# The written order of a feed-forward: GELUs and high halves behind the bank copies, another order of one pop, a second ring for one sum, low halves moved

## The chip, the core and the metric

The kernel runs on one core of a Trainium2 chip. A core has TensorE (PE; its weight loads are listed apart as PEld), VectorE (DVE), ScalarE (ACT), GpSimd (POOL) and SyncE (SP), each with its own in-order queue; they meet through semaphores. Matrix products go from on-chip memory (SBUF) into eight accumulation banks (PSUM) of 128 x 512 fp32 words. The metric is the device time of one execution in microseconds; lower is better.

## What is computed

One transformer block on 2048 rows of width 512, with a modulation vector that gives a shift, a scale and a gate for each of its two halves:

```python
x = A_x
sa, ca, ga, sb, cb, gb = silu(c) @ w_mod             # six vectors of 512
h = layernorm(x) * (1 + ca) + sa
x = x + ga * attention(h, k_cache, v_cache, wq, wo)  # 32 heads of 128, 512 keys
h = layernorm(x) * (1 + cb) + sb
x = x + gb * ((gelu(h @ w_gate) * (h @ w_up)) @ w_down)   # hidden width 1792
```

Inputs and outputs are fp32.

## The kernel before

**Precision.** TensorE works on fp16. Each fp32 operand is held as a *high half* (the value rounded to fp16) and a *low half* (the rest), and each product is three matmuls: low x high, high x high, high x low (`mm3`, L86, whose matmuls stand at L90). So every result that feeds another product costs ScalarE one copy to fp16 (the high half) and VectorE or GpSimd one subtraction (the low half).

**Stages.** Attention takes the first three quarters of the time. The feed-forward follows, in an order written out by hand: under `manual_schedule` each engine executes its instructions in the order in which the Python code emits them. The loop at the end of the kernel is that order (L1756 to L1777).

**The feed-forward's steps.** The hidden width is 14 tiles of 128 features, taken in pairs, and the rows are taken in two halves of 1024. That gives 14 values of n: 7 pairs for the first half of the rows (n = 0 to 6), then 7 for the second. Step q = 2n + m computes the gate projection (m = 0) or the up projection (m = 1) of pair n: two feature tiles by two blocks of 512 rows, four output tiles named "11", "12", "21", "22". It does so with seven block products instead of eight (a Strassen-like scheme), in the written order `ORDER` = 1, 2, 6, 7, 5, 4, 3. A *product* here is two groups of three matmuls into one bank. `CHAIN` (L865) tells the bank: products 1, 6, 7 and 4 pile up in bank a, 2 goes to bank b, 5 and 3 to bank c.

Since 1, 6, 7 and 4 add onto the same bank a, its state must be copied out between them: after 1 as "s1", after 6 as "u2", after 7 as "u3" (`keep`, a ScalarE copy at L885). The product that follows in bank a waits for that copy. Then VectorE adds: "11" = s1 + bank b, "22" = u3 + bank c after product 5, "12" = u2 + bank c after product 3 (L1270), and "21" is bank a itself after product 4.

**What becomes of the four tiles.** In a gate step (m = 0) each gets its GELU on ScalarE (`gelu`, L1276), straight after it is formed. In an up step (m = 1) VectorE multiplies gate by up (L1287). The result is the input of the down projection, in one of two forms:

- For n mod 7 in 5, 6 (`turned(n)` false) `parts` makes high and low halves of the four tiles (L1297, L1301) and the down projection is eight plain row blocks.
- For n mod 7 in 0 to 4 (`turned(n)` true) the down projection is again a seven-product scheme, and needs besides "11", "21", "22" four combinations: `sums_of` makes four subtractions on GpSimd (L1313), named t1, t3, t2, t4 in the order of the code, and then their high halves on ScalarE (L1297) and low halves on GpSimd (L1301).

**put_off and tick.** `put_off(n, fn)` lays a piece of work aside, and `tick()`, which runs once after each product, emits it at the n-th tick from then. Pieces due at the same tick come in the order in which they were laid aside. The counters given in `sums_of`, (high, low) = (2, 4), (3, 5), (3, 4), (4, 5), are such delays. Since `sums_of` is called in the last product of step 2n+1, a delay of 2 means behind the first product of step 2n+2, 3 behind its second, and so on.

**Pops.** The down projection's work is queued in `nexty`; `y_next()` takes a *pop* off it, six matmuls, at four places of a step: after the products 2, 6, 4 and 3 (k = 1, 2, 5, 6 in the loop). For a turned n, `yt_tasks` writes 14 groups of three matmuls, two times seven products in the order `YORDER`, and cuts them into seven pops. The pops of n begin in step 2n+2 after its third product: (1,2), (6,5), (7,3), (4,1'), (2',6'), (5',7'), (4',3'), a prime marking the second seven. They use banks ya, yb, yc by the same `CHAIN`, and behind every group VectorE adds the bank to an accumulator (`yt_add`, L1677, and L1680 where it is the first). A group that adds onto a bank waits for that read.

**Buffers.** `tmp` (L74) hands out tiles of a ring of six ("e"). In a gate step `place` gives such a tile to s1, u2 and u3, and the GELU of "21" takes one more; they are free again only when the low halves of t1 to t4, made in place of them, have been read, one gate step later. `place` has a test `k == 6`, but it is called with the names "s1", "u2", "u3".

**Others in the same queues.** During steps 2 to 6 the second half's layer norm runs beside the products (`ln_turned`): per 128 rows a normalization and a high half on ScalarE (L539, L543), a low half on GpSimd (L544), then a transposing DMA; `turned_out` writes its results with ScalarE and VectorE (L558, L559). During steps 8 to 13 `combos` makes the input combinations for the second half: high halves on ScalarE (L374), low halves and subtractions on GpSimd (L378, L574).

Of the kernel before, what the change touches and what calls it, by code (L numbers as in the profile page):

```python
# [10 lines left out]
F32 = mybir.dt.float32  # L11
# [4 lines left out]
ALU = mybir.AluOpType  # L16
AX = mybir.AxisListType

P = 128
# [6 lines left out]
QB = 512  # L26
# [38 lines left out]
def block_kernel(ctx: ExitStack, tc: tile.TileContext, x, kT, v, wq, wo, wg, wu, wd, cT, wc, wm, out):  # L65
    nc = tc.nc

    const = ctx.enter_context(tc.tile_pool(name="const", bufs=1))
    pool = ctx.enter_context(tc.tile_pool(name="pool", bufs=2))
# [4 lines left out]
    def tmp(name):  # L74
        return pool.tile([P, 512], F32, tag="e", name=name, bufs=NE)

    def raw(name):
        return pool.tile([P, 512], F32, tag="raw", name=name, bufs=NRAW)

    def pair(tag, name, bufs):  # L80
        return pool.tile([P, 2, 512], F16, tag=tag, name=name, bufs=bufs)
# [12 lines left out]
    def dma(out_, in_):  # L94
        moved[0] += 1
        nc.sync.dma_start(out_, in_)
# [81 lines left out]
    def col(name, i=0):  # L178
        return ST[name][:, i:i + 1]
# [113 lines left out]
    def turned(n):  # L293

        return n % NP < NP - NROW
# [159 lines left out]

    def put_off(n, fn):

        waits_.append([n, fn])

    def tick():  # L460
# [68 lines left out]
    def ln_turned(i):  # L529

        qb, i_ = divmod(i, QT)
        st = {}

        def load():
            st["x"] = raw("xs")
            dma(st["x"], y1[2 * QT + i])

        def norm():
            nc.scalar.activation(st["x"], st["x"], AF.Identity, bias=col("kinv", i), scale=col("kmax", i))  # L539

        def split():
            st["p"] = t = pool.tile([P, 2, W], F16, tag="p16", name="xh", bufs=NP16)
            nc.scalar.activation(t[:, 0, :], st["x"], AF.Copy)  # L543
            nc.gpsimd.tensor_tensor(t[:, 1, :], st["x"], t[:, 0, :], op=ALU.subtract)  # L544

        def turn():
            if i_ == 0:
                TURN[qb] = pool.tile([P, QT, 2 * KT, P], F16, tag="pt", name="xt", bufs=NPT)
            nc.sync.dma_start_transpose(TURN[qb][:, i_], st["p"].rearrange("p a b -> p (a b)"))

        return load, norm, split, turn
# [182 lines left out]
    def run(key):  # L734
        for fn in later.pop(key, []):
            fn()
# [130 lines left out]
    def with_posts(key, gen, bk, after):  # L867
        items = {}
        for k, (b, start) in CHAIN.items():
            g0, g1 = product(key, gen, k, bk(b), start, k in (2, 4, 3))  # L870
            items[k] = [g0, (g1[0], lambda k=k: after(k))]
        return items

    def banks(st, tags):
        def bk(k):
            def get():
                if k not in st:
                    st[k] = bank(*tags[k])
                return st[k]
            return get  # L880
        return bk

    def keep(st, k, t):
        st[k] = t
        nc.scalar.activation(t, st["a"], AF.Copy)  # L885

    def kept(k):
        return pool.tile([P, QB], F32, tag=k, name=k, bufs=1)
# [364 lines left out]
    NQ = 4 * NP  # L1253
# [7 lines left out]
    def f_scale(q):  # L1261
        return (q // 2) % NP * 2 + q % 2

    def f_items(q, hold=None):
        n, m = divmod(q, 2)
        st = {}
        done = set()

        def add(k, src):
            nc.vector.tensor_tensor(st[k], st[k], st[src], op=ALU.add)  # L1270

        def gelu(key, src):

            def apply():
                dst = tmp("fg") if key == "21" else src
                nc.scalar.activation(dst, src, AF.Gelu_apprx_tanh, scale=col("finv", f_scale(q)))  # L1276
                G[n, key] = dst

            return (apply,)

        def result(key, src):
            if m == 0:
                for step in gelu(key, src):
                    step()
            else:
                g = G[n, key]
                nc.vector.scalar_tensor_tensor(g, g, col("gsc", n % NP), src, op0=ALU.mult, op1=ALU.mult)  # L1287
                if not turned(n):
                    parts(key, G.pop((n, key)))
                elif key != "12":  # L1290
                    parts(key, g)
                else:
                    sums_of()

        def high_of(key, g):
            t = A[n, key] = pair("ot", "at", NOT)
            nc.scalar.activation(t[:, 0, :], g, AF.Copy)  # L1297

        def low_of(key, g, eng):
            t = A[n, key]  # L1300
            eng.tensor_tensor(t[:, 1, :], g, t[:, 0, :], op=ALU.subtract)  # L1301

        def parts(key, g):
            high_of(key, g)
            if key == "21":
                st["low"] = lambda: low_of(key, g, nc.vector)
            else:
                put_off(2, lambda: low_of(key, g, nc.vector))

        def sums_of():  # L1310
            g = {k: G.pop((n, k)) for k in ("11", "12", "21", "22")}
            for o, a, b in (("11", "12", "11"), ("12", "22", "12"), ("22", "22", "11"), ("21", "21", "22")):
                nc.gpsimd.tensor_tensor(g[o], g[a], g[b], op=ALU.subtract)  # L1313
            for key, o, high, low in (("t1", "11", 2, 4), ("t3", "12", 3, 5), ("t2", "22", 3, 4), ("t4", "21", 4, 5)):
                put_off(high, lambda key=key, o=o: high_of(key, g[o]))
                put_off(low, lambda key=key, o=o: low_of(key, g[o], nc.gpsimd))

        def out_(key, src):
            if not hold:
                result(key, src)  # L1320
            else:
                hold.append(gelu(key, src))

        def place(k):
            if m == 0:
                return pool.tile([P, QB], F32, tag="k", name="fg", bufs=2) if k == 6 else tmp("fg")
            return pool.tile([P, QB], F32, tag="p16", name="fu", bufs=NP16) if k == "s1" else kept(k)

        def after(k):
            done.add(k)  # L1330
            if k in (1, 6, 7):
                name = {1: "s1", 6: "u2", 7: "u3"}[k]
                keep(st, name, place(name))
            if k == 2:
                add("s1", "b")
                out_("11", st["s1"])
            elif k == 4:
                out_("21", st["a"])
            elif k == 3:
                if "low" in st:  # L1340
                    st["low"]()
                add("u2", "c")
                out_("12", st["u2"])
            if k in (5, 7) and {5, 7} <= done:
                add("u3", "c")
                out_("22", st["u3"])

        tags = {"a": ("s", "fa", 2) if q else ("qa", "fa", 1), "b": ("acc", "fb", NACC), "c": ("acc", "fc", NACC)}
        return with_posts(("f", q), 2 + q // (2 * NP), banks(st, tags), after)
# [168 lines left out]
    def items(g):  # L1518
        if g not in ITEMS:
            ITEMS[g] = q_items(g) if g < NG else f_items(g - NG, hold)  # L1520
        return ITEMS[g]
# [104 lines left out]
    def f_at(q, k, *fns):  # L1626
        at(("f", q, k), *fns)
# [8 lines left out]
    def step(q, fn):  # L1636
        f_at(q // 7, q % 7, fn)
# [9 lines left out]
    for p in range(2):  # L1647
        q = 61 + 14 * p
# [69 lines left out]
            del YR["t", qb]  # L1718

    ADDS = {1: ((0, 0),), 2: ((0, 0),), 6: ((0, 1),), 5: ((1, 1),), 7: ((1, 1),), 4: ((1, 0),), 3: ((0, 1),)}  # L1720
    YORDER = ((1, 2, 6, 5, 7, 3, 4), (1, 2, 6, 5, 7, 4, 3))
    LAST = {2: (0, 0), 7: (1, 1), 3: (0, 1), 4: (1, 0)}

    def yt_tasks(n):
        tasks = []
        for p in range(2):
# [21 lines left out]

            tasks += [(lambda k=k, f=group: f(k), lambda k=k, f=post: f(k)) for k in YORDER[p]]
        return [tasks[k:k + 2] for k in range(0, len(tasks), 2)]  # L1750
# [5 lines left out]
    for q in range(NQ):  # L1756
        n, m = divmod(q, 2)
        its = items(NG + q) if q < 2 else f_items(q)
        for k, pk in enumerate(ORDER):
            if (q, pk) not in f_done:  # L1760
                all_of(its[pk])
            run(("f", q, k))
            tick()
            if n and k == 2 and m == 0 and turned(n - 1):
                nexty += yt_tasks(n - 1)
            if k in ((1, 2, 5, 6) if q < NQ - 1 else (1, 5)):
                y_next()
        if m == 1 and not turned(n):
            for qi, (a, b) in enumerate((("11", "21"), ("12", "22"))):
                for i in range(QT):  # L1770
                    nexty.append(y_tasks((2 * (n // NP) + qi) * QT + i, [lambda n=n, a=a: A[n, a], lambda n=n, b=b: A[n, b]],
                                         [("f", n, 0), ("f", n, 1)], col("dysc", n % NP), f_final))
# [40 lines left out]
```

## Time and profile before

| | |
|---|---|
| time, median of 3 runs | 1762.55 us (1762.18 to 1762.99) |
| the profiled execution | 1762.83 us, its span 1761.0 us |
| granted TensorE clock, mean | 0.998 |
| feed-forward, step 2 to the last product | from 1359.5 us on |

How to read the lines that follow. A line of the timeline begins with its start in microseconds from the span's beginning and its length, then the engine, the source line, the operation, output<-input by the program's names, sizes, and how many instructions were merged; a bracket gives the idle time of that engine just before and what ended it. fa, fb, fc are the banks of a feed-forward product; ya, yb, yc those of a pop of a turned n, py those of a pop of rows; fg and u are the gate and up tiles, at the halves that feed the down projection, yt its accumulators, xs and xh the layer norm's tile and halves. A line of the waits names who waited for whom, the total in us, how often, and the longest. A line of a group has its count, busy time and mean in ns, and the idle time before its instructions with what ended it.

### The profile page before, as it was taken

The numbers are of one execution on the slowest core, as the hardware profiler recorded it, in microseconds if no ns is written. First come the engines' busy times: TensorE is split into PE (matmuls) and PEld (weight loads), VectorE is DVE, ScalarE is ACT, GpSimd is POOL, SyncE is SP. The second block draws the span as 40 slices with busy tenths as digits, with TensorE's granted clock in tenths as the row PEclk, the third lists the DMA queues.
The fourth block names the chain that finished last, engine by engine and source line by source line (L and its number), as shares of the span: only waits on it lengthen the run. The fifth ranks groups of instructions, "written<-read, shape, count | busy, mean of one in ns | idle before, by whom it ended". The sixth has DMA issues, their size and how long they took to land.

```text
span 1761.0 us, 26246 instructions
## 1 busy us (share of the span) xinstructions
PE 1718.3 (98%) x8020; PEld 788.1 (45%) x8022; DVE 1415.7 (80%) x2454; ACT 1242.6 (71%) x2797; POOL 1063.9 (60%) x1282
## 2 busy tenths in 40 slices
PE   7999999999999999999999999999999998999998
PEld 5444444444444444444444444444444343444443
DVE  7898898888888899888888888888876575656665
ACT  6988888888878777887778778787773544433342
POOL 4889777777788874745585584574512536642424
PEclk9999999999999999999999999999999999999999
DMA  7999999999999999999999999999985544743353
GB/s 238 216 203 212 212 217 204 224 215 215 218 213 228 205 208 185 206 212 234 209 202 240 219 198 229 208 216 206 212 152 159 137 144 151 181 142 98 96 154 97
DMA packets 690637, 339.83 MB, mean 193 GB/s; under 512 B 578880, under 2 KB 601408, under 8 KB 690496
## 3 DMA queue, kind: packets, MB, share of 16 engines
q1 hardware_dynamic: 690208, 337.63, 84.6%
q8 instruction: 63, 1.03, 0.2%
q14 instruction: 78, 0.64, 0.1%
q10 hardware_dynamic: 288, 0.52, 0.1%
HBM read 135.66 MB, written 61.87 MB: 112 GB/s over the span
## 4 chain that ended last, share of the span: by engine, by line
PE 83%; DVE 7%; ACT 5%; POOL 2%; issue 2%; DMA 1%; DVEq 0%; SPq 0%; POOLq 0%; ACTq 0%
PE py L90 19%; PE ps L90 17%; PE po L90 17%; PE qa L90 8%; PE fa L90 6%; PE qc L90 4%; PE fc L90 3%; PE ya L90 2%; PE qb L90 2%; PE fb L90 2%; ACT ee L991 1%; PE yc L90 1%; ACT p L1003 1%; PE pq L90 1%; DVE nm L982 1%
## 5 line engine op out<-in xcount | busy, mean ns | idle before, releaser
L991 ACT ACTIVATE ee<-ps,nm 128x512 f32<-128x512 f32 x512 | 349.8, 683 | 188.0 <-DVE nm L982 183.6
L1008 DVE SCALAR_TENSOR_TENSOR p<-ee,rr,p 128x512 f16<-128x512 f32 x512 | 459.0, 897 | 6.0 <-ACT p L1003 5.5
L982 DVE TENSOR_REDUCE nm<-ps 128x1 f32<-128x512 f32 x512 | 350.1, 684 | 105.0 <-PE ps L90 102.3
L90 PE MATMUL ps<-k,qt 128*128 128x512 f16 x1536 | 414.9, 379 | 5.6 <-ACT ee L991 4.5
L1003 ACT ACTIVATE p<-ee,rr 128x512 f16<-128x512 f32 x512 | 364.5, 712 | 23.4 <-DMA pt<-p 10.8
L90 PE MATMUL po<-pt,v 128*128 128x512 f16 x1536 | 372.9, 379 | 1.8 <-DMA pt<-p 1.8
L90 PE MATMUL py<-wo,ot 128*128 128x512 f16 x1536 | 371.5, 379 | 0.1
L90 PEld LDWEIGHTS <-w 128*128 128x128 f16 x2184 | 213.8, 98 | 272.6 <-issue 16.9
L90 PEld LDWEIGHTS <-v 128*128 128x128 f16 x1536 | 149.9, 98 | 184.1 <-DMA pt<-p 2.0
L90 PEld LDWEIGHTS <-ot 128*128 128x128 f16 x1536 | 150.2, 98 | 181.7 <-DVE ot L740 0.5
L90 PEld LDWEIGHTS <-qt 128*128 128x128 f16 x1536 | 145.9, 98 | 177.0 <-issue 4.5
L1313 POOL TENSOR_TENSOR fg<-fg 128x512 f32<-128x512 f32 x40 | 51.9, 1298 | 151.5 <-DVE fg L1287 149.1
L740 DVE SCALAR_TENSOR_TENSOR ot<-po,ot 128x512 f16<-128x512 f32 x128 | 87.7, 685 | 37.4 <-ACT ot L739 37.0
L1297 ACT ACTIVATE at<-fg 128x512 f16<-128x512 f32 x86 | 53.3, 626 | 79.2 <-DVE fg L1287 74.3
L991 ACT ACTIVATION_READ_ACCUMULATOR ee<-ps,nm 128x1 f32 x512 | 100.0, 195 | 0.0
L952 DVE SCALAR_TENSOR_TENSOR acc<-py,ysc,acc 128x512 f32<-128x512 f32 x128 | 94.7, 740 | 5.3 <-PE py L90 5.3
L90 PE MATMUL fa<-t,w 128*128 128x512 f16 x336 | 81.6, 379 | 11.2 <-ACT fg L885 10.2
L235 POOL TENSOR_TENSOR lw<-lw,half__86 128x1 f32<-128x1 f32 x37 | 22.9, 619 | 104.2 <-DVE lw L185 104.2
L90 PE MATMUL qa<-t,w 128*128 128x512 f16 x348 | 84.9, 379 | 0.0
L397 POOL TENSOR_TENSOR rs<-rs,nhalf 128x1 f32<-128x1 f32 x32 | 18.7, 584 | 101.9 <-DVE rs L391 99.0
L739 ACT ACTIVATE ot<-po 128x512 f16<-128x512 f32 x128 | 73.7, 576 | 5.0 <-PE po L90 5.0
L90 PE MATMUL ya<-at,wo 128*128 128x512 f16 x240 | 63.9, 382 | 6.5 <-DVE yt L1677 6.5
(241 smaller groups left out, 2765.2 us busy)
## 6 DMA issues: line engine op xcount, KB each, us to landing
w<-kept SPq DMA_DIRECT2D x123, 256.0 KB, 3.3
wo<-kept SPq DMA_DIRECT2D x70, 256.0 KB, 3.4
kept<-stage SPq DMA_DIRECT2D x61, 256.0 KB, 3.4
raw<-in_wo SPq DMA_DIRECT2D x56, 256.0 KB, 3.2
kept<-w SPq DMA_DIRECT2D x39, 256.0 KB, 3.4
rw<-in_wq SPq DMA_DIRECT2D x38, 256.0 KB, 3.1
hs<-hf SPq DMA_DIRECT2D x32, 256.0 KB, 2.8
pt<-p SPq DMA_TRANSPOSE x512, 3.5
```

What stands on the lines that cost most here:

```text
L90: nc.tensor.matmul(ps, a, b, start=first and n == 0, stop=last and n == 2, skip_group_check=chain)
L235: nc.gpsimd.tensor_tensor(out, out, half_, op=ALU.pow)
L397: nc.gpsimd.tensor_tensor(st["rs"], st["rs"], nhalf, op=ALU.pow)
L739: nc.scalar.activation(t[:, 0, :], src, AF.Copy, scale=scale)
L740: return lambda: nc.vector.scalar_tensor_tensor(t[:, 1, :], src, scale, t[:, 0, :], op0=ALU.mult, op1=ALU.subtract)
L952: nc.vector.scalar_tensor_tensor(acc[ti], st["p"], by, acc[ti], op0=ALU.mult, op1=ALU.add)
L982: nc.vector.tensor_reduce(nm, E[t]["ps"], axis=AX.X, op=ALU.max, negate=True)
L991: nc.scalar.activation(e, E[t]["ps"], AF.Exp, bias=E[t]["nm"], scale=1.0, accum_out=sm[:, t % 2:t % 2 + 1])
L1003: nc.scalar.activation(p16[:, 0, :], E[t]["e"], AF.Copy, scale=E[t]["r"])
L1008: nc.vector.scalar_tensor_tensor(p16[:, 1, :], E[t]["e"], E[t]["r"], p16[:, 0, :], op0=ALU.mult, op1=ALU.subtract)
L1297: nc.scalar.activation(t[:, 0, :], g, AF.Copy)
L1313: nc.gpsimd.tensor_tensor(g[o], g[a], g[b], op=ALU.subtract)
```

## The change

```diff
@@ put_off @@
+        if n == 0:
+            return fn()
         waits_.append([n, fn])
@@ ln_turned: split @@
             nc.scalar.activation(t[:, 0, :], st["x"], AF.Copy)
-            nc.gpsimd.tensor_tensor(t[:, 1, :], st["x"], t[:, 0, :], op=ALU.subtract)
+            put_off(2, lambda: nc.vector.tensor_tensor(t[:, 1, :], st["x"], t[:, 0, :], op=ALU.subtract))
@@ f_items: result @@
             if m == 0:
-                for step in gelu(key, src):
-                    step()
+                put_off(2 if key == "11" else 0, gelu(key, src)[0])
@@ f_items: parts @@
-                put_off(2, lambda: low_of(key, g, nc.vector))
+                put_off(3 if key == "11" else 2, lambda: low_of(key, g, nc.vector))
@@ f_items: sums_of @@
-            for key, o, high, low in (("t1", "11", 2, 4), ("t3", "12", 3, 5), ("t2", "22", 3, 4), ("t4", "21", 4, 5)):
-                put_off(high, lambda key=key, o=o: high_of(key, g[o]))
-                put_off(low, lambda key=key, o=o: low_of(key, g[o], nc.gpsimd))
+            late = 0 if n else 2
+            for key, o, high, low in (("t1", "11", 2, 5), ("t3", "12", 3, 6), ("t2", "22", 4, 5), ("t4", "21", 5, 6)):
+                put_off(high + (late if high < 5 else late // 2), lambda key=key, o=o: high_of(key, g[o]))
+                put_off(low + late // 2, lambda key=key, o=o: low_of(key, g[o], nc.gpsimd))
@@ f_items: place @@
-                return pool.tile([P, QB], F32, tag="k", name="fg", bufs=2) if k == 6 else tmp("fg")
+                return pool.tile([P, QB], F32, tag="k", name="fg", bufs=2) if k == "u2" and n else tmp("fg")
@@ the pops @@
-    YORDER = ((1, 2, 6, 5, 7, 3, 4), (1, 2, 6, 5, 7, 4, 3))
+    YORDER = ((1, 2, 6, 5, 7, 3, 4), (1, 2, 6, 7, 5, 4, 3))
@@ the loop of the feed-forward @@
-            if k in ((1, 2, 5, 6) if q < NQ - 1 else (1, 5)):
+            if k in ((1, 2, 5, 6) if q < NQ - 1 else (2, 5)):
                 y_next()
```

In words: the layer norm's low half moves from GpSimd to VectorE and two ticks back. In a gate step the GELU of "11" is emitted two ticks later, which is behind the copy u2. The high halves of t2 and t4 come one tick later, the low halves of all four too; for n = 0 the highs of t1, t3 and t2 come two ticks later still and the high of t4 and all lows one. The low half of "11" comes one tick later. u2 of a gate step gets a ring of its own, the two buffers "k" that held attention's keys (not for n = 0). In the second seven of a turned n the groups 5' and 7' change places. In the last step the first pop moves from behind product 2 to behind product 6.

## The prediction

> **What bounds the kernel now.** I read the page's busy shares first, then busy time by stretches, then the waits of the feed-forward, then its timeline.
>
> ```profile
> span 1761.0 us, 26246 instructions
> ...
> PE 1718.3 (98%) x8020; PEld 788.1 (45%) x8022; DVE 1415.7 (80%) x2454; ACT 1242.6 (71%) x2797; POOL 1063.9 (60%) x1282
> ```
>
> TensorE is the bound, so the change can only return time in which TensorE stands still or runs slowly. To find it I cut the feed-forward into periods: from product 1 of an even step q to product 1 of step q+2.
>
> ```profile
> 1359.48:1391.89 32.41, 29.20 (x127) 12.76 (x126) 19.07 (x29) 15.86 (x26) 13.00 (x11) 0.95 0.51 148
> 1391.89:1421.07 29.18, 27.67 (x127) 12.30 (x126) 19.46 (x29) 16.58 (x27) 14.13 (x12) 1.00 0.61 158
> 1421.07:1451.11 30.04, 27.68 (x128) 12.29 (x127) 22.23 (x33) 14.51 (x23) 11.51 (x9) 1.00 0.43 131
> 1451.11:1481.19 30.08, 27.52 (x128) 12.33 (x127) 20.73 (x30) 12.25 (x21) 15.51 (x12) 1.00 0.64 201
> 1481.19:1515.73 34.54, 29.42 (x127) 12.74 (x126) 18.64 (x28) 17.78 (x28) 25.78 (x21) 0.95 0.59 148
> 1515.73:1573.04 57.31, 57.14 (x266) 25.83 (x265) 33.98 (x46) 22.03 (x35) 28.12 (x21) 1.00 0.46 135
> 1573.04:1601.77 28.73, 27.51 (x127) 12.33 (x126) 17.78 (x27) 10.31 (x17) 9.54 (x8) 1.00 0.41 130
> 1601.77:1630.55 28.78, 27.52 (x128) 12.30 (x127) 18.49 (x28) 10.41 (x17) 9.54 (x8) 1.00 0.32 98
> ```
>
> The columns are the stretch and its length, then busy time (and count) of PE, PEld, DVE, ACT, POOL, then the granted clock. A product and a pop are six matmuls each, and six take 1.295 us (starts 1597.07 to 1598.37 and 1600.48 to 1601.77 in the rows below). A period with seven pops is 21 x 1.295 = 27.2 us; the stretch from 1515.73 holds two with eight pops each, 57.0. So the periods lose 5.2 (q=2), 2.0 (q=4), 2.85 (q=6), 2.9 (q=8), 7.35 (q=10), 0.3 (q=12 to 15), 1.55 (q=16) and 1.6 us (q=18; I take q=20, 22, 24 to be alike). With the last step's 1.1 that is about 29.6 us: all there is to win.
>
> ```profile
> PE fa L90 <- ACT fg L885: 14.7, 14, 3.4
> ...
> ACT fg L885 <- POOL at L1301: 8.0, 3, 5.0
> ...
> PE ya L90 <- DVE yt L1677: 6.5, 10, 0.7
> ...
> PE fa L90 <- ACT u L885: 1.0, 1, 1.0
> ```
>
> Two waits fill it: products wait for ScalarE's copy of bank a (L885), and pops wait for a VectorE add (L1677). Printed idle is some 0.16 us below the lost time, since a matmul's modelled end overlaps the next start; I count from start to start.
>
> **The pop order** (YORDER). Around a pop of step 17:
>
> ```profile
> 1597.07 0.81 PE L90 MATMUL yc<-at,wo 128*128 128x512 f16 x3
> ...
> 1597.72 0.81 PE L90 MATMUL ya<-at,wo 128*128 128x512 f16 x3
> ...
> 1598.37 1.46 PE L90 MATMUL fc<-b,w 128*128 128x512 f16 x6
> 1598.83 0.74 DVE L1680 TENSOR_SCALAR yt<-yc,dyc 128x512 f32<-128x512 f32 x1
> 1599.67 0.75 DVE L1677 SCALAR_TENSOR_TENSOR yt<-ya,dyc,yt 128x512 f32<-128x512 f32 x1
> ...
> 1600.48 0.81 PE L90 MATMUL ya<-at,wo 128*128 128x512 f16 x3 [0.65 <-DVE yt L1677]
> ```
>
> Group 5 (yc) and group 7 (ya) are followed by group 4, which adds onto bank a and so waits until VectorE has read 7. TensorE was ready at 1598.37+1.295 = 1599.66 and lost 0.81. Swapped, 7's add takes the place at 1598.83 and lets group 4 go at 1598.83+0.81 = 1599.64: no wait. Group 3 is late next: it adds onto bank c, whose read now runs 1599.67 to 1600.42, so it starts at 1600.48 instead of 1600.31. The loss goes from 0.81 to 0.17, ten times: 6.4 us (between 0, if the adds fall further behind, and 8.1).
>
> **GELU and high halves behind the copies.** Step 18:
>
> ```profile
> 1601.77 1.46 PE L90 MATMUL fa<-b,w 128*128 128x512 f16 x6
> 1602.55 5.31 POOL L1313 TENSOR_TENSOR fg<-fg 128x512 f32<-128x512 f32 x4 [19.00 <-DVE fg L1287]
> ...
> 1605.35 0.72 ACT L1276 ACTIVATE fg<-fg,finv 128x512 f32<-128x512 f32 x1 [0.86 <-DVE fg L1270]
> ...
> 1605.98 1.20 ACT L1297 ACTIVATE at<-fg 128x512 f16<-128x512 f32 x2
> ...
> 1607.09 0.58 ACT L885 ACTIVATE fg<-fa 128x512 f32<-128x512 f32 x1
> ...
> 1607.72 1.46 PE L90 MATMUL fa<-t,w 128*128 128x512 f16 x6 [0.61 <-ACT fg L885]
> 1607.82 4.50 POOL L1301 TENSOR_TENSOR at<-fg,at 128x512 f16<-128x512 f32 x4
> ```
>
> POOL's subtractions start at P = 1602.55, 1.33 apart. ScalarE's queue is GELU, high of t3, high of t2, copy u2; t2's high waits for the third subtraction (P+3.99 = 1606.54), the copy follows at 1607.09 and product 7 at P+5.17. TensorE could have gone at 1601.77+4x1.295 = 1606.95. Afterwards only t3's high stands ahead of the copy, and waits for the second subtraction: P+2.66 = 1605.21, copy 0.55 later, product 7 another 0.63 later, P+3.84 = 1606.39. P hangs on VectorE's queue, in which the pop swap exchanges two adds of one length, so P stays while TensorE comes 0.64 earlier: 0.08 is left. This period goes from 1.6 to 0.08+0.17 = 0.25, and so four times: 5.4 us. In q=16 no such pop stands before it, and only the 0.17 stays: 1.4.
>
> The GELU then runs where ScalarE waits for TensorE, and its result is used a step later. The low halves stay covered: POOL ends four subtractions at P+5.3 and two lows at P+7.6, while the pop with groups 6 and 5 needs t2's low in its third matmul, P+3.84+3x1.295+0.43 = P+8.15. That is a slack of 0.55 us; uncovered, each microsecond of lag costs one per period.
>
> **The second ring.** Of the three waits of the copy u3 for POOL's lows (8.0 us), 5.0 lie in q=10 and the others in q=4 and 6. The tmp ring has six buffers and held four tiles of each n; with u2 elsewhere it holds three, so u3 no longer meets a tile whose low half is pending. What is left in q=4, 6 and 8 is the bound by P.
>
> ```profile
> 1421.79 5.72 POOL L1313 TENSOR_TENSOR fg<-fg 128x512 f32<-128x512 f32 x4 [7.80 <-DVE fg L1287]
> ...
> 1451.89 6.02 POOL L1313 TENSOR_TENSOR fg<-fg 128x512 f32<-128x512 f32 x4 [18.36 <-DVE fg L1287]
> ```
>
> I leave 0.25 in q=4, 0.5 in q=6 and 0.8 in q=8, because the four subtractions last 0.4 (q=6) and 0.7 us (q=8) longer than 5.31, and half of that lies ahead of t3's high. Gains: 1.75, 2.35, 2.1.
>
> **The layer norm's low half goes to VectorE.**
>
> ```profile
> L544 POOL TENSOR_TENSOR xh<-xs,xh 128x512 f16<-128x512 f32 x8 | 9.2, 1155 | 16.3 <-ACT xh L543 11.5 <-issue 4.7
> ...
> L1301 DVE TENSOR_TENSOR at<-fg,at 128x512 f16<-128x512 f32 x43 | 30.7, 714 | 0.7
> ...
> L1270 DVE TENSOR_TENSOR fg<-fg,fc 128x512 f32<-128x512 f32 x26 | 17.9, 687 | 45.5 <-PE fc L90 35.0 <-ACT fg L885 10.5
> ```
>
> Eight times 1.16 us leave POOL and eight times 0.71 enter VectorE, 5.7 us, beside 45.5 us in which it idles ahead of one add alone. Bounds 0 and 5.7; I take 0.5, for step 5, where this half, the moved low of "11" and a layer-norm output all come ahead of the add of u3. The low of "11" elsewhere only shifts within that idle time.
>
> By the Trainium skill (GPSIMD Engine Reference, section 8, Key points) GpSimd shares its SBUF interfaces with VectorE and contends with VectorE instructions that have two SBUF inputs, which the moved half is: it would stretch the subtractions of q=4 and q=6, some 0.3 us each by my estimate, and the sum would be 0.6 worse. The trace bears it out only as far as the subtractions' lengths differ (5.31 in q=18).
>
> **The first pop of sums** (n=0, q=2):
>
> ```profile
> 1362.21 5.31 POOL L1313 TENSOR_TENSOR fg<-fg 128x512 f32<-128x512 f32 x4 [4.61 <-DVE fg L1287]
> ...
> 1366.75 0.58 ACT L885 ACTIVATE fg<-fa 128x512 f32<-128x512 f32 x1
> ...
> 1367.38 1.48 PE L90 MATMUL fa<-t,w 128*128 128x512 f16 x6 [2.56 <-ACT fg L885]
> ...
> 1368.67 2.74 PE L90 MATMUL fc<-t,w 128*128 128x512 f16 x6
> ```
>
> The copy again trails t2's high, and behind the stall six matmuls take 2.54 us (1368.67 to 1371.21), half speed: 2.7 of the 5.2 us are the wait, the rest the clock and one pop wait. With the highs two pops later, products 7, 5 and 4 run unhindered from 1359.48+4x1.295 = 1364.66, and the pop with groups 6 and 5 is due at 1368.55. Now t2's high is late: it stands behind the GELU of "22", which needs product 5 (ends near 1367.4), an add and itself 0.7 each: high 1368.9 to 1369.5, low on POOL until 1370.7, third matmul due at 1368.98. It loses 1.75, with the swap's 0.17 1.9 in all: 3.3 us gained.
>
> **Step 10**, where POOL also makes the next block's combinations:
>
> ```profile
> 1491.91 2.27 POOL L1301 TENSOR_TENSOR at<-fg,at 128x512 f16<-128x512 f32 x2
> ...
> 1493.10 0.60 ACT L885 ACTIVATE fg<-fa 128x512 f32<-128x512 f32 x1 [5.02 <-POOL at L1301]
> ...
> 1494.14 1.16 POOL L378 TENSOR_TENSOR t<-cb,t 128x512 f16<-128x512 f32 x1
> ...
> 1495.09 1.49 PE L90 MATMUL ya<-at,wo 128*128 128x512 f16 x3
> ```
>
> The ring's 5.0 us go, but the same lows are what the pop at 1495.09 reads. They move one tick back, behind the L378 of 1494.14 (1.1 us): t2's low ends at 1491.91+1.1+2.3 = 1495.3. TensorE, unhindered, is there at 1481.19-0.64+7x1.295+0.08 = 1489.7, its third matmul at 1490.1: a stall of 5.2 us, and half speed behind it (three matmuls in 1.49 against 0.81 now; 3.4 us at half speed are 1.7). Loss 7.2 after 7.35: next to nothing gained.
>
> By the Trainium skill (TensorE: Matmul & The Clock Gate, Part 1) the clock halves after one idle window of about 3.4 us on a free-running grid. The trace shows half speed after a wait of 2.56 already, so I charge it; by the rule a stall of 5.2 covers a whole window only about half the time, an estimate, and the sum would be 0.9 better.
>
> **The rest.** Steps 12 to 15: 0.3, as the copy no longer follows the GELU. Last step: its second pop moves between products 6 and 7 and covers the copy (1.0 printed): 1.1.
>
> **Sum**: 5.4 + 1.4 + (1.75 - 0.5) + 2.35 + 2.1 + 3.3 + 0.15 + 0.3 + 1.1 = 17.3 us, so a span of 1743.7. The profiled execution took 1762.83, 1.8 over its span and 0.3 over the median of the runs: 1745.
>
> **Rivals.**
> (a) Step 10's stall does not come, because POOL passes its combinations faster when the layer norm is off it: 6.9 more, 1738. For it: 5 us of ring wait vanish. Against it: POOL is busy 25.78 of 34.54 us there, and the layer norm's halves are mostly gone by then.
> (b) The copies stay tied to P+5.2, because VectorE brings the second subtraction or the GELU's input later; then the pop swap is swallowed too, and only n=0, the ring, steps 12 to 15 and the last step pay: some 6 us, 1756. Against it: the GELU is no longer ahead of the copy.
> (c) Slower: t2's low, moved back a tick, comes late at the pop with groups 6 and 5 in all eight ordinary periods. The slack is 0.55; with a lag of 3.5 us beyond it and half speed behind each stall (1.7), 8 x 5.2 - 17 = 24 us lost, 1787; it decides from a lag of about 2.7 (2.1 us a period, before the clock). For it: step 10 shows POOL's queue doing this once. Against: the other periods have POOL busy 9.5 to 15.5 us of 30.
> (d) No effect that can be told: the second ring could be a dead test, as the old one is (place gets "u2", never 6), but the new one compares names, and the swaps are plain.
>
> **Chances**: forecast 0.70, (a) 0.12, (b) 0.11, (c) 0.05, (d) 0.02. The forecast's own spread, from 0 to 8.1 for the swap, 0 to 5.7 for the halves and 0 to 1.7 for a clock drop in q=2, is about 1740 to 1750; (a) takes the range down to 1738, part of (b) up to 1753. A measurement here tells 0.2%, 3.5 us, from no change: faster 0.93, same 0.02, slower 0.05.
>
> **What would show it.** Right: the ten waits of ya on L1677 gone or replaced by about 0.0 to 0.2 ahead of yc; product 7 at P+3.8 in steps 18 to 24, the wait for L885 down from 14.7 to 2 or less; no L885 waiting on L1301; one wait of ya near step 10 on POOL's L1301 of about 5 us, with the clock at half behind it; in step 2 one of 1 to 2 us in the pop. Wrong: product 7 still at P+5, a new wait of pops on L1301 in ordinary periods, or VectorE late at the add of u3.

## The result and the profile after

The changed kernel takes 1748.13 us (median of 4 runs, 1746.52 to 1749.16), the kernel before 1762.77 us (4 runs, 1762.18 to 1763.44): 14.6 us less. The ratio is 0.9916 with a 95% interval of 0.9899 to 0.9933. The prediction was 1745, with a range of 1738 to 1753. The profiled execution took 1748.16 us, its span 1745.9 us, so 15.1 us of span went.

The waits of TensorE in the feed-forward of the changed kernel, all that the view lists (who waited for whom, us in total, times, longest). Lines of the source have moved by up to two: L887 is the copy of bank a, L1302 the low halves, L1298 the high halves.

```profile
PE ya L90 <- POOL at L1302: 5.7, 2, 5.1
PE ya L90 <- ACT at L1298: 0.8, 1, 0.8
PE fa L90 <- ACT fg L887: 0.8, 3, 0.3
PE fa L90 <- ACT u L887: 0.4, 1, 0.4
```

The 14.7 us of waiting for the copy are 0.8, the ten waits for VectorE's add are gone from the list, and one wait of 5.1 us for a low half on GpSimd is new. Busy time by the same stretches as before (product 1 of an even step to product 1 two steps on):

```profile
1360.43:1389.58 29.15, 27.67 (x127) 12.33 (x126) 20.80 (x31) 15.54 (x26) 9.59 (x8) 1.00 0.57 162
1389.58:1417.34 27.76, 27.51 (x127) 12.33 (x126) 21.74 (x33) 16.47 (x27) 10.34 (x8) 1.00 0.64 166
1417.34:1445.36 28.02, 27.68 (x128) 12.32 (x127) 23.59 (x34) 14.29 (x23) 10.66 (x8) 1.00 0.50 141
1445.36:1473.16 27.80, 27.51 (x127) 12.33 (x126) 20.77 (x30) 12.37 (x21) 15.52 (x12) 1.00 0.67 210
1473.16:1507.84 34.68, 29.58 (x127) 12.77 (x126) 18.68 (x28) 18.13 (x28) 25.20 (x21) 0.90 0.59 144
1507.84:1565.19 57.35, 57.21 (x266) 25.82 (x264) 34.34 (x47) 21.92 (x35) 28.30 (x21) 1.00 0.48 140
1565.19:1592.55 27.36, 27.35 (x127) 12.34 (x126) 17.26 (x26) 10.40 (x17) 9.55 (x8) 1.00 0.41 130
1592.55:1619.99 27.44, 27.43 (x128) 12.31 (x126) 18.54 (x28) 10.40 (x17) 9.56 (x8) 1.00 0.34 101
```

The first number after the stretch is its length. Every period but that of step 10 and the long one has moved closer to the 27.2 us that its 21 groups of six matmuls need. The gains, before minus after: 3.3 (step 2), 1.4, 2.0, 2.3, -0.1 (step 10), 0.0 (steps 12 to 15), 1.4 (step 16), 1.3 in each of the four periods from step 18 to step 25. From step 26 to the end it is 0.5. That is 16.0 us; 0.95 are lost before step 2 (it begins at 1360.43 instead of 1359.48), where the change moves no more than one low half. In the kernels run below that start lies between 1359.5 and 1361.7; the kernel with the pop order alone, which changes nothing ahead of step 2, begins it at 1360.73.

The timeline of the changed kernel around a pop and the step behind it:

```profile
1589.79 1.46 PE L90 MATMUL fc<-b,w 128*128 128x512 f16 x6
1590.25 0.75 DVE L1682 TENSOR_SCALAR yt<-ya,dyc 128x512 f32<-128x512 f32 x1
1591.09 0.81 PE L90 MATMUL ya<-at,wo 128*128 128x512 f16 x3
1591.10 0.75 DVE L1679 SCALAR_TENSOR_TENSOR yt<-yc,dyc,yt 128x512 f32<-128x512 f32 x1
...
1591.90 0.81 PE L90 MATMUL yc<-at,wo 128*128 128x512 f16 x3
...
1592.55 1.46 PE L90 MATMUL fa<-b,w 128*128 128x512 f16 x6
...
1593.98 5.33 POOL L1314 TENSOR_TENSOR fg<-fg 128x512 f32<-128x512 f32 x4 [18.27 <-DVE fg L1288]
...
1596.64 0.63 ACT L1298 ACTIVATE at<-fg 128x512 f16<-128x512 f32 x1 [0.72 <-POOL fg L1314]
...
1597.17 0.58 ACT L887 ACTIVATE fg<-fa 128x512 f32<-128x512 f32 x1
...
1597.81 1.46 PE L90 MATMUL fa<-t,w 128*128 128x512 f16 x6
1597.99 0.63 ACT L1298 ACTIVATE at<-fg 128x512 f16<-128x512 f32 x1 [0.24 <-POOL fg L1314]
1598.53 0.70 ACT L1278 ACTIVATE fg<-fg,finv 128x512 f32<-128x512 f32 x1
```

Group 4 (ya, 1591.09) starts 1.30 behind product 3, so without a wait. Group 3 (yc, 1591.90) starts 0.81 behind it instead of 0.65: the read of bank c by the add at 1591.10 costs it 0.16. On ScalarE the copy (1597.17) stands right behind the high half of t3, and the high half of t2 and the GELU follow it. Product 7 comes at 1597.81, which is P+3.83 with P = 1593.98.

In step 12 a copy that prepares an accumulator's transpose (L1698) stands ahead of the copy of bank a, and product 7 starts 1.60 behind the pop's 1513.09 instead of 1.295:

```profile
1513.09 1.46 PE L90 MATMUL py<-wo,at 128*128 128x512 f16 x6
1513.11 1.05 ACT L1698 ACTIVATE yu<-yt 128x1024 uint16<-128x1024 uint16 x1
...
1514.06 0.58 ACT L887 ACTIVATE fg<-fa 128x512 f32<-128x512 f32 x1
...
1514.69 1.46 PE L90 MATMUL fa<-t,w 128*128 128x512 f16 x6
```

### The profile page after: what moved, and what is told of

It is laid out like the page before. It is cut to its first block, busy times and chain, and to the rows that moved or that the text cites. A ratio compares the mean times of both kernels' runs of the same rounds, so it can differ in the third digit from the quotient of the medians.

```text
span 1745.9 us, 26253 instructions
## 1 busy us (share of the span) xinstructions
PE 1716.3 (98%) x8022; PEld 787.6 (45%) x8022; DVE 1423.4 (82%) x2462; ACT 1243.0 (71%) x2797; POOL 1056.9 (61%) x1274
## 4 chain that ended last, share of the span: by engine, by line
PE 85%; DVE 5%; ACT 4%; POOL 2%; DMA 2%; issue 1%; SPq 0%; POOLq 0%; DVEq 0%; ACTq 0%
PE py L90 19%; PE po L90 17%; PE ps L90 17%; PE qa L90 8%; PE fa L90 7%; PE qc L90 4%; PE fc L90 4%; PE ya L90 2%; PE qb L90 2%; PE fb L90 2%; DMA pt<-p 1%; PE yc L90 1%; ACT ee L993 1%; ACT p L1005 1%; PE pq L90 1%
## 5 line engine op out<-in xcount | busy, mean ns | idle before, releaser
L742 DVE SCALAR_TENSOR_TENSOR ot<-po,ot 128x512 f16<-128x512 f32 x128 | 87.8, 686 | 36.7 <-ACT ot L741 36.3
L1298 ACT ACTIVATE at<-fg 128x512 f16<-128x512 f32 x86 | 53.9, 627 | 88.8 <-DVE fg L1288 75.0
```

The source lines that it names most:

```text
L742: return lambda: nc.vector.scalar_tensor_tensor(t[:, 1, :], src, scale, t[:, 0, :], op0=ALU.mult, op1=ALU.subtract)
```

## The experiments

Two theories were to be told apart. By the *chain*, product 7 is tied to P, the start of the subtractions, and P to VectorE; the parts of the change then only work together. By the rival, each part removes its own wait and the gains add up. Lengths of the periods in us (start of product 1 to start of product 1; 27.2 is the least, 57.0 for the long one), from the profiles:

| period from step | 2 | 4 | 6 | 8 | 10 | 12 to 15 | 16 | 18 |
|---|---|---|---|---|---|---|---|---|
| before | 32.4 | 29.2 | 30.0 | 30.1 | 34.5 | 57.3 | 28.7 | 28.8 |
| after | 29.15 | 27.8 | 28.0 | 27.8 | 34.7 | 57.35 | 27.4 | 27.4 |
| pop order alone | 30.1 | 29.2 | 30.0 | 30.1 | 34.5 | 57.95 | 28.1 | 28.8 |
| after, old pop order | 29.8 | 28.0 | 28.0 | 28.0 | 34.85 | 57.0 | 28.0 | 28.0 |
| after, without second ring | 31.1 | 28.5 | 29.2 | 28.8 | 36.3 | 57.3 | 27.4 | 28.15 |
| after, old GELU and halves | 30.1 | 29.1 | 31.7 | 31.8 | 33.45 | 58.0 | 28.1 | 28.8 |
| after, layer norm's halves back | 29.3 | 29.35 | 28.8 | 27.8 | 35.4 | 57.3 | 27.4 | 27.4 |
| after, late = 0 | 28.7 | 27.75 | 28.0 | 27.8 | 34.1 | 57.35 | 27.4 | 27.4 |
| after, lows of n=4 on VectorE | 29.15 | 27.75 | 28.0 | 27.8 | 28.9 | 57.3 | 27.4 | 27.4 |
| the same, t2's high earlier | 28.7 | 27.75 | 28.0 | 27.8 | 29.1 | 57.35 | 27.4 | 27.4 |

### The pop order alone

```diff
 # the kernel before
-    YORDER = ((1, 2, 6, 5, 7, 3, 4), (1, 2, 6, 5, 7, 4, 3))
+    YORDER = ((1, 2, 6, 5, 7, 3, 4), (1, 2, 6, 7, 5, 4, 3))
```

> The kernel before with the new pop order alone (5' and 7' exchanged), nothing else of the change. Theory of the chain: product 7 of a gate step is bound by P, the start of GpSimd's subtractions, and P hangs on VectorE, which the swap does not shorten. So TensorE gains 0.64 us at each of ten pops and gives it back at product 7 in all periods whose sums follow; only the pops of n=4 and n=11 keep it: 1.3 us, about 1761.4. The wait of ya for L1677 goes, the wait of fa for L885 grows from 14.7 to about 20 us, product 7 stays at P+5.2 in steps 18 to 24. Rival, the parts add up: ten times 0.64 to 0.81, 6.4 to 8.1 us, 1755 to 1756, with the wait for L885 unchanged.

Measured: 1762.00 us against 1762.84 for the kernel before; ratio 0.9998, interval 0.9989 to 1.0007. The waits of TensorE and step 18 of this kernel:

```profile
PE fa L90 <- ACT fg L885: 20.4, 14, 3.9
...
1602.13 5.31 POOL L1313 TENSOR_TENSOR fg<-fg 128x512 f32<-128x512 f32 x4 [19.00 <-DVE fg L1287]
...
1607.31 1.46 PE L90 MATMUL fa<-t,w 128*128 128x512 f16 x6 [1.26 <-ACT fg L885]
```

No wait for an add is left, the wait for the copy has grown from 14.7 to 20.4 us, and product 7 stands at P+5.18. The wait before it is 1.26 where it was 0.61. P has not moved with TensorE: it lies 1.43 us behind product 1 (1600.70), where it lay 0.78 behind it. The periods of steps 4, 6, 8, 10 and 18 are what they were to a tenth; that of step 16, with no new pop ahead of it, keeps 0.64, and the long period ahead of step 16 is 0.64 longer. The 2.3 us of step 2 are for the most part half speed that the profile of before has and this one has not (shown in the last section). The sum theory falls.

### The changed kernel with the old pop order

```diff
 # the changed kernel
-    YORDER = ((1, 2, 6, 5, 7, 3, 4), (1, 2, 6, 7, 5, 4, 3))
+    YORDER = ((1, 2, 6, 5, 7, 3, 4), (1, 2, 6, 5, 7, 4, 3))
```

> The changed kernel with the old pop order. Theory of the chain: with the copies no longer behind the GELU the swap is worth 0.56 us in each ordinary period (0.81 lost against 0.08 plus 0.17), 0.64 for n=4 and n=11, nothing where step 10 follows: about 5.2 us, 1753.3. Product 7 in steps 18 to 24 comes without a wait. Rival, the parts add up: the same 6.4 to 8.1 as alone, 1754.5 to 1756. The two theories part by the difference to the swap alone: 1.3 against 5.2 for the chain, equal for the rival.

Measured: 1751.46 us, ratio to the kernel before 0.9938 (0.9925 to 0.9950), 3.3 us slower than the changed kernel. The intervals of the two ratios overlap; the lowest of the runs here, 1750.78, lies above the highest of the changed kernel, 1749.16. Step 18:

```profile
1596.19 5.33 POOL L1314 TENSOR_TENSOR fg<-fg 128x512 f32<-128x512 f32 x4 [18.27 <-DVE fg L1288]
...
1600.59 1.46 PE L90 MATMUL fa<-t,w 128*128 128x512 f16 x6
```

Product 7 has no wait at all here, and steps 18 to 24 take 28.0 instead of 27.4 us: 0.57 each, against 0.56 expected. Steps 2 and 16 lose 0.65 each, but steps 4, 6 and 8 only 0.25, 0.0 and 0.2, where the slower subtractions leave the rest of the gain to P, and the long period is even 0.4 shorter: behind n=4 the swap is not kept. That is why the sum stays below 5.2. So one and the same edit is worth nothing that can be told alone (0.8 us between the medians) and 3.3 us with the rest.

### The changed kernel without the second ring

```diff
 # the changed kernel, place(), m == 0
-                return pool.tile([P, QB], F32, tag="k", name="fg", bufs=2) if k == "u2" and n else tmp("fg")
+                return tmp("fg")
```

> The changed kernel with u2 of the gate steps in the common ring of six again. Theory of the chain: copy u3 then waits in every period for the low half of t1 on GpSimd, which now ends near P+6.5 while the copy would be due at P+5.4; product 4 comes at P+7.1 instead of P+6.4. Seven periods with 0.7 us, 4.9 us, about 1753; the wait of fa for L885 near 5 to 6 us, L885 waiting for L1301's low on GpSimd in each gate step. Rival: the ring only mattered where the kernel before showed the wait, in steps 4 and 6: 1.4 us, 1749.5.

Measured: 1757.53 us, ratio to before 0.9968 (0.9955 to 0.9980), 9.4 us slower than the changed kernel. Step 18:

```profile
1599.64 5.33 POOL L1314 TENSOR_TENSOR fg<-fg 128x512 f32<-128x512 f32 x4 [18.36 <-DVE fg L1288]
...
1606.12 0.60 ACT L887 ACTIVATE fg<-fa 128x512 f32<-128x512 f32 x1 [1.22 <-POOL at L1302]
...
1606.77 1.46 PE L90 MATMUL fa<-t,x 128*128 128x512 f16 x6 [0.55 <-ACT fg L887]
```

The copy u3 waits for a low half on GpSimd, and product 4 comes at P+7.13 (P+7.1 expected): 0.7 us in steps 4 and 18 to 24, 1.2 and 1.0 in steps 6 and 8. The ring is thus more than a remedy for the three waits that the profile of before showed: it is what lets the later low halves be late. The expectation was still too small: it left out step 2 (31.1 against 29.15), where u3 of n=1 needs the tile of n=0 whose low comes late on purpose, and step 10 (36.3 against 34.7), where product 4 waits 6.3 us for the copy. Steps 6 and 8 are dearer than the 0.7 reckoned, too.

### The changed kernel with the old places of GELU and halves

```diff
 # the changed kernel
-                put_off(2 if key == "11" else 0, gelu(key, src)[0])
+                put_off(0, gelu(key, src)[0])
...
-            late = 0 if n else 2
-            for key, o, high, low in (("t1", "11", 2, 5), ("t3", "12", 3, 6), ("t2", "22", 4, 5), ("t4", "21", 5, 6)):
+            late = 0
+            for key, o, high, low in (("t1", "11", 2, 4), ("t3", "12", 3, 5), ("t2", "22", 3, 4), ("t4", "21", 4, 5)):
```

> The changed kernel with the GELU of 11 and the halves of t1 to t4 emitted where they were before (also for n=0); pop order, second ring, layer norm's low half and low half of 11 as changed. Theory of the chain: product 7 is back at P+5.2 (1.33 us in seven periods, 0.8 in step 16) and step 2 loses 3.3: 13.4 us, about 1761.5, so that nearly the whole gain goes although three of the parts stay. Rival, the parts add up: only the waits for L885 of before come back, some 9 to 11 us, 1757 to 1759, and the pop order's 6.4 us stay.

Measured: 1763.58 us, ratio to before 1.0000 (0.9991 to 1.0009). Step 18, and product 7 of step 8:

```profile
1603.97 5.32 POOL L1314 TENSOR_TENSOR fg<-fg 128x512 f32<-128x512 f32 x4 [19.00 <-DVE fg L1288]
...
1606.12 0.72 ACT L1278 ACTIVATE fg<-fg,finv 128x512 f32<-128x512 f32 x1 [0.22 <-DVE fg L1272]
...
1607.97 0.63 ACT L1298 ACTIVATE at<-fg 128x512 f16<-128x512 f32 x1 [0.61 <-POOL fg L1314]
...
1609.14 1.46 PE L90 MATMUL fa<-t,w 128*128 128x512 f16 x6 [1.26 <-ACT fg L887]
```

```profile
1459.18 2.63 PE L90 MATMUL fa<-t,w 128*128 128x512 f16 x6 [2.55 <-ACT fg L887]
```

Pop order, second ring and layer norm's halves are as changed, and nothing of the gain is left: product 7 is again at P+5.2 (1.26 us of wait in step 18) and the periods of steps 16 and 18 are those of the pop order alone. Steps 6 and 8 are even 1.7 us longer than before; their waits reached 2.5 us and matmuls at half speed followed. Without these 3.4 us this kernel would lie some 2.6 us below the kernel before, whose own profile has 1.7 us of the kind in step 2. The lines also tell which of the moved pieces holds up the copy: the high half of t2 waits for the third subtraction until 1607.97, when the GELU has been over for more than a microsecond. GELU and high halves were not run apart.

### The layer norm's low halves back on GpSimd

```diff
 # the changed kernel, split()
-            put_off(2, lambda: nc.vector.tensor_tensor(t[:, 1, :], st["x"], t[:, 0, :], op=ALU.subtract))
+            nc.gpsimd.tensor_tensor(t[:, 1, :], st["x"], t[:, 0, :], op=ALU.subtract)
```

> The changed kernel with the layer norm's low halves on GpSimd again, at their old place. Theory: GpSimd then has one such half of 1.16 us ahead of the lows of t1 and t2 in steps 2 and 6 and two in step 4, with a slack of 0.55 us: the pop with groups 6 and 5 waits 1.75 us in step 4, 0.6 in step 6, 0.3 more in step 2, in all 2.6 us slower than the changed kernel, about 1750.8. Rival, as the record has it: the move only costs VectorE time (0.5 us in step 5) and saves nothing, so that undoing it gives 1747.6.

Measured: 1750.23 us, ratio to before 0.9926 (0.9914 to 0.9939), 2.1 us slower than the changed kernel. Step 4:

```profile
1397.87 1.16 POOL L546 TENSOR_TENSOR xh<-xs,xh 128x512 f16<-128x512 f32 x1 [0.24 <-ACT xh L545]
...
1398.98 4.50 POOL L1302 TENSOR_TENSOR at<-fg,at 128x512 f16<-128x512 f32 x4
1401.31 0.38 PE L90 MATMUL ya<-at,wo 128*128 128x512 f16 x1 [1.82 <-POOL at L1302]
```

The third matmul of the pop waits 1.8 us for t2's low; the periods of steps 4 and 6 are 1.6 and 0.8 us longer, near the 1.75 and 0.6 expected. (The 0.7 of step 10 are half speed behind the same wait of 5.08 us.) The move is a part with a gain of its own, and the prediction had entered it as a cost. What it costs can be seen on GpSimd, in the four subtractions of step 4, first of the changed kernel and then of this one:

```profile
1391.01 5.66 POOL L1314 TENSOR_TENSOR fg<-fg 128x512 f32<-128x512 f32 x4 [17.11 <-DVE fg L1288]
```

```profile
1391.18 5.33 POOL L1314 TENSOR_TENSOR fg<-fg 128x512 f32<-128x512 f32 x4 [7.84 <-DVE fg L1288]
```

### Without the later places for n=0

```diff
 # the changed kernel, sums_of()
-            late = 0 if n else 2
+            late = 0
```

> The changed kernel without the later places for n=0 (late = 0). Theory, from the changed kernel's rows: product 7 of step 2 then waits for the high of t3, P+3.84, which is 1.4 us late, but the pop with groups 6 and 5 meets its halves; the period goes from 29.15 to about 28.7, the time to about 1747.7, no difference that can be measured. Rival: the delay is what saves step 2; without it 3.3 us come back there (period 32.4), 1751.4.

Measured: 1747.83 us, ratio to before 0.9913 (0.9899 to 0.9926). The period of step 2 takes 28.7 instead of 29.15 us, as expected. What saves step 2 is the order of copy, halves and GELU (at their old places product 7 waits 2.56 us there); the extra delay for n=0 is not needed, and no difference in time can be told.

### The lows of n=4 on VectorE

```diff
 # the changed kernel, sums_of()
-                put_off(low + late // 2, lambda key=key, o=o: low_of(key, g[o], nc.gpsimd))
+                put_off(low + late // 2, lambda key=key, o=o: low_of(key, g[o], nc.vector if n == 4 else nc.gpsimd))
```

> The changed kernel with the four low halves of t1 to t4 of n=4 alone on VectorE instead of GpSimd. Theory: step 10 stands still only because its lows queue on GpSimd behind four operations of the next block's combinations; VectorE has idle time there. The stall of 5.1 us and the half speed behind it go, the period falls from 34.7 to about 27.5, the time to about 1741 (7 us below the changed kernel). Rival: the pop also waits for ScalarE's high halves, or the lows on VectorE delay its add of u3, and no more than 3 us are gained: 1745.

Step 10 of the changed kernel first:

```profile
1483.35 1.26 POOL L576 TENSOR_TENSOR cb<-cb 128x512 f32<-128x512 f32 x1
1484.57 1.15 POOL L378 TENSOR_TENSOR t<-cb,t 128x512 f16<-128x512 f32 x1
...
1485.68 4.47 POOL L1302 TENSOR_TENSOR at<-fg,at 128x512 f16<-128x512 f32 x4
1487.98 0.59 PE L90 MATMUL ya<-at,wo 128*128 128x512 f16 x1 [5.09 <-POOL at L1302]
1488.37 1.48 PE L90 MATMUL yc<-at,wo 128*128 128x512 f16 x3
```

The lows stand last in GpSimd's row of operations, and the pop's third matmul waits 5.09 us for the second of them. With these four on VectorE the time is 1742.03 us, ratio to before 0.9880 (0.9865 to 0.9896): 6.1 us below the changed kernel. The period falls to 28.9 us, the clock in it is granted in full, and what is left of the stall is:

```profile
L1302 DVE TENSOR_TENSOR at<-fg,at 128x512 f16<-128x512 f32 x4 | 5.3, 1372 | 0.0
L576 POOL TENSOR_TENSOR cb<-cb 128x512 f32<-128x512 f32 x2 | 3.4, 1714 | 0.0
...
1485.61 0.81 PE L90 MATMUL ya<-at,wo 128*128 128x512 f16 x3 [0.94 <-DVE yt L1679]
```

(the first two lines are groups of that kernel from 1478 to 1486 us: busy time and mean ns). It stopped 1.4 us short of 27.5. The lows took 1372 ns each on VectorE, where the mean in the kernel before is 714, and held up the adds of the pop: the wait of 0.94 us is about 1.1 from start to start. The rest is small waits.

### The same, and t2's high for n=0 one tick earlier

```diff
 # the kernel of the last experiment, sums_of()
-                put_off(high + (late if high < 5 else late // 2), lambda key=key, o=o: high_of(key, g[o]))
+                put_off(high + (late if high < 4 else late // 2), lambda key=key, o=o: high_of(key, g[o]))
```

> The changed kernel with the lows of n=4 on VectorE and, for n=0, the high half of t2 one tick earlier (5 instead of 6, ahead of the GELU of 22). Theory: as without the second edit, and in step 2 the pop waits only for t2's low behind t1's, 0.85 us instead of 1.75: period 28.1, the time 0.9 below the first edit alone, about 1740. Rival: t2's high ahead of the GELU of 22 holds up that chain and the period stays at 29.1 or grows.

Measured: 1741.12 us, ratio to before 0.9876 (0.9863 to 0.9890), the fastest of all. The period of step 2 is 28.7 us, 0.5 less and not 1.0: the pop still waits 1.1 us for t2's low on GpSimd. The difference between the two last kernels, 0.9 us, is no more than their runs scatter.

## Why the prediction was right, point by point

- **What bounds**: TensorE's lost time in the feed-forward, 29.6 us of it. Right: the gain came out of this lost time, 16.0 us of it.
- **The pop order**, 0.81 to 0.17 at each pop, with group 3 late next. Right in mechanism and size (0.16 in the timeline). The period behind n=4 did not keep it, though: with the old order it is 0.4 shorter.
- **GELU and high halves**, product 7 from P+5.2 to P+3.84, P unmoved by the swap. Right: P+3.83, four periods of 1.34 us gained where 1.35 were forecast. That the swap is worth nothing that can be told without this part is shown by the two runs of the pop order and by the run with the old places.
- **The second ring**, priced by three waits. Its gain in the sum came out, but its role was under-read: without it a wait of the copy u3 costs time in steps 2 to 10 and 18 to 24.
- **The layer norm's half**, charged with 0.5. Wrong in sign: it is worth about 2 us, since the lows behind it on GpSimd had only 0.55 us to spare. The prediction had that slack in its sum and did not put the old half of 1.16 us against it. The price named in its place is there: the four subtractions of steps 4 and 6 last 5.66 and 5.98 us where they lasted 5.31 and 5.72, and with this half back on GpSimd, all else as changed, they last 5.33 and 5.74: that is some 0.3 us each, as estimated. The Trainium skill (GPSIMD Engine Reference, section 8, Key points) says that GpSimd shares its SBUF interfaces with VectorE; these lengths agree with it.
- **Step 2**, 1.9 left. Right: 29.15 of 27.2, in the two waits foretold, for t2's high (0.83) and its low (0.64). Some 1.7 us of the 3.3 gained are the half speed of the profile of before, which a run need not have (below): that part of the gain is luck.
- **Step 10**, the ring's wait replaced by one of the pop on GpSimd, no gain. Right: a wait of 5.09 us against 5.2, and a period of 34.7 against 34.4 (27.2 and a loss of 7.2). That the time agrees so closely is in part luck, since behind a wait of 5.08 us the run with late = 0 has a period of 34.1. Moving only these lows returns 6 us, so it was GpSimd's queue.
- **Steps 12 to 15**, 0.3, and the **last step**, 1.1: mis-sized, 0.0 and 0.5. The copy still trails other work of ScalarE there. In step 12 the GELU stands behind the copy now, but a copy of an accumulator (L1698, 1.05 us) ahead of it, and product 7 starts 0.31 late as it did before (0.33). In the last step product 7 started 1.14 late and now 0.60, behind a high half that waits for VectorE. (The pop moved there is the first of its two; the prediction calls it the second.)
- **The sum**: 17.3 forecast, 16.0 found in the feed-forward, 15.1 in the span. Of the missing 2.2 us, 0.95 lie before step 2, no more than other kernels differ there, 0.3 in step 10, 0.3 in the long period and 0.6 in the end.

The rivals: (a) step 10 free, (b) the copies tied to P+5.2 and (c) lows late in all periods did not come. (b) describes the run of the pop order alone, and (c) what the moved layer norm's halves prevent: with them back on GpSimd the pop of step 4 waits 1.8 us. (d) is out, too: without the second ring 9.4 us go. The later low half of "11" and the moved pop of the last step were not run by themselves.

## What to carry to other kernels

Where a queue in written order feeds a bound engine, an edit is worth what the next release after it allows: measure each release from the event that sets it (here P), not from the engine that waits, and the swallowed edits show beforehand. Before a half or a copy is made later, list every buffer that its reader still holds, and every queue entry that stands ahead of it. A wait that vanishes where one engine works without a gap, as GpSimd in the first half of step 10's period, can reappear at the next reader of its results; there less work on that engine helped.

## What the runs showed of the hardware

**The same wait with and without half speed.** Step 2 of the kernel before and of the pop order alone, after waits of 2.56 and 2.55 us:

```profile
1367.38 1.48 PE L90 MATMUL fa<-t,w 128*128 128x512 f16 x6 [2.56 <-ACT fg L885]
1368.67 2.74 PE L90 MATMUL fc<-t,w 128*128 128x512 f16 x6
```

```profile
1368.63 1.46 PE L90 MATMUL fa<-t,w 128*128 128x512 f16 x6 [2.55 <-ACT fg L885]
1369.92 1.46 PE L90 MATMUL fc<-t,w 128*128 128x512 f16 x6
```

Six matmuls take 2.54 us in the one and 1.29 in the other. Behind the stall of step 10, 5.09 us in the changed kernel and 5.08 with late = 0, the mean granted clock of the period is 0.90 and 0.95, and the periods are 34.7 and 34.1 us. The Trainium skill (TensorE: Matmul & The Clock Gate, Part 1) gives the idle window a free-running grid; that like stalls cost differently in these pairs agrees with it. The 3.4 us that it wants idle do not agree: a wait of 2.56 us was enough here. What makes the runs of one kernel scatter was not shown: the changed kernel's lie within 2.6 us, those of the two kernels without step 10's stall within 1.0 and 2.5.

**VectorE and GpSimd side by side.** The low half of a tile takes VectorE 714 ns on average, and 1372 ns in step 10 beside GpSimd's combinations; the subtractions among those (L576) took 1714 ns there instead of 1260. Work moved from a busy GpSimd to VectorE at this place cost almost twice its time on VectorE, and GpSimd's own subtractions a third more.
